# The MLP's first pair: rows for LayerNorm loaded later, LayerNorm two half steps later, weight parts in smaller portions

## The chip, the cores and the metric

The kernel runs on one core of a Trainium2 chip. The metric is device time in microseconds (us) of one execution, the median of several runs. A core has five instruction queues that run side by side and wait for each other through semaphores: TensorE (PE in the profile: matmuls; PEld is its load of the stationary operand), VectorE (DVE), ScalarE (ACT), GpSimd (POOL) and SyncE (SP, which here only issues DMA transfers). Each queue runs its instructions in order: one that waits holds up all that stand behind it on the same engine.

## The reference

A transformer block with S = 2048 tokens, D = 640 features, F = 1728 hidden features, all in float32. Attention is linear attention; after it comes the MLP, which is where the change lies. Cut to what matters:

```python
x = x + ga * attention(layernorm(x) * (1 + ca) + sa)
h = layernorm(x) * (1 + cb) + sb
r = relu(h @ w1 + b1)
x = x + gb * ((r * r) @ w2 + b2)
```

`sa, ca, ga, sb, cb, gb` are six rows made from a conditioning vector.

## The kernel before

**Tiles.** The 2048 tokens are 8 pairs `j` of two tiles of 128 tokens; the F features are 14 blocks `f` of 128 (the last one 64), taken two at a time in 7 steps `n`. Every float32 operand of a matmul is split into a high and a low part (`hi`, a copy on ScalarE, and `lo`, a subtraction on VectorE, line 88), and each product is made of three matmuls.

**The MLP loop.** For every pair and step it runs two half steps. The half step `2n` has `up(j, 2n)` (15 matmuls of `w1` with the normed tokens, into PSUM), then ScalarE's relu with bias (line 1184) and VectorE's square (line 1185); then `down(0)`, the first half of the products of the step before with `w2`. The half step `2n+1` has `up(j, 2n+1)`, relu, square, then `split_a` (lines 1208 and 1214 on ScalarE, line 88 on VectorE), which writes the split activations `ra`, then `down(1)`. So a `down` of step `n` reads the `ra` that the half step before it made. The order on all engines is the order of this code: pairs 0 and 1 are written with a manual schedule, which in pair 0 holds for SP too.

**Weight parts.** While pair 0 runs, the rest of the weights is still being loaded and split. The list `preps` has 28 parts, numbered from 0 in its order (blocks of `w1` and `w2` in turn; 14 is w1_9, 15 w2_5, 16 w1_10, 17 w2_6, 18 w1_11, 19 w2_7, 20 w1_12, 21 w2_8, 22 w1_13, 23 w2_9, 24 to 27 w2_10 to w2_13). When the MLP begins, 14 are loaded and 9 are split. `prep(n)`, called once in every half step with the next number of `PREPS`, does for the next `n` parts: the high copy on ScalarE (line 953), the low subtraction on VectorE (line 88), and issues `n` further loads on SP (lines 943 and 946, 320 KB each). The raw rows lie in a ring `s1` of five buffers, so a load waits until VectorE is done with an older row. The split weights of w1_13 (part 22) have no place of their own and take a buffer of the same ring.

**LayerNorm of the next pair.** `layer(j + 1, at)` is called in every half step `at` of pair `j` and runs what a table lists for it. For pair 1 the table is `LN_AT0`. Its entries: `load` is the half step in which SP issues the two loads of attention's rows (`xm`, line 1005) and, unless `xx` says otherwise, the two of x's rows (`xx`, line 1015), 320 KB each; `add` the half steps of the two additions on VectorE (line 1019; SP then stores the sum, line 1020); `ln` the half steps of six pieces on ScalarE: two sums (line 1418), two sums of squares (line 1423), two scalings (line 1430), with small POOL instructions between them (lines 1420 to 1427); and the keys 10, 11 and 12 the half steps in which TensorE transposes the normed tokens (`t2`, line 364, output `tb`) and ScalarE and VectorE scale and split them (lines 375, 376, 88) for pair 1's `up`. The PSUM tile that `tb` goes to exists once. In an even half step of pair 0, `t2`, loads and additions stand between `down(0)` and `prep`, and the pieces of `ln` behind `prep`; in an odd one all of `layer` stands behind `prep`.

Of the kernel before, what the change touches and what calls it, by code (L numbers as in the profile page):

```python
# [51 lines left out]
def kernel(  # L52
# [1210 lines left out]
    def t_split(n):  # L1263

        a, b = TR_[n]
        for r, w in (("a", a[:, L]), ("b", TR_[n, "b"][:, 1].bitcast(F32)), ("c", b[:, L]), (None, b[:, R])):
            if r == "b":
                t = TR_[n, "b"]
            elif r and n == NP - 2:
                at = 512 if r == "a" else 1280  # L1270
                t = TR_["end"][:, at : at + 768].rearrange("p (s n) -> p s n", s=2)
            else:
                t = ring(r, f"tst{n}_{r}") if r else W2[2 * n][:, :, R]
            nc.scalar.activation(t[:, 0], w, AF.Copy)
            lo(t[:, 1], w, t[:, 0])
            if r:
                nc.sync.dma_start(TD[n][r], t.bitcast(F32))
# [121 lines left out]
    def prep(n):  # L1399
        p_hi(n)  # L1400
        p_lo(n)
        p_load(n)
# [1 line left out]
    prev = None  # L1404
    LN2 = {}

    LN_AT0 = {"load": 1, "add": (4, 5), "ln": (4, 5, 6, 7, 8, 9), 10: (0, 1), 11: (2, 3), 12: (4,)}
    LN_AT1 = {"load": 3, "add": (5, 5), "ln": (5, 6, 6, 7, 8, 8), 9: (0, 1), 11: (2, 3), 12: (4,)}
    LN_AT2 = {"load": 0, "xx": 3, "add": (6, 7), "ln": (7, 8, 8, 8, 9, 9), 10: (0, 1), 11: (2, 3), 12: (4,)}
    LN_AT = {"load": 0, "add": (3, 4), "ln": (4, 5, 6, 6, 7, 7), 8: (0, 1), 10: (2, 3), 12: (4,)}  # L1410
    PREPS = iter([1, 3] + [2, 2] * 2 + [2, 1] * 2 + [1])

    def ln_pieces(xt, nm, spare):
        sm = small([P, 2], "sm", f"sm{nm}")
# [18 lines left out]
    def layer(j, at, part=None):  # L1433
        todo = {1: LN_AT0, PLAIN: LN_AT1, PLAIN + 1: LN_AT2}.get(j, LN_AT)
        if j == NB:
            return
        if part != 1:
            if at in todo:
                t2(j, *todo[at])
            if todo["load"] == at:  # L1440
                load_xm(j)
            if todo.get("xx", todo["load"]) == at:
                load_xx(j)
            for i in range(2):
                if todo["add"][i] == at:
                    add_x(j, i)
        if part == 0:
            return
        for i in range(6):
            if todo["ln"][i] == at:  # L1450
                if i == 0:
                    LN2[j] = ln_pieces(XM[j], f"b{j}", XX[j])
                next(LN2[j])

    for j in range(NB):
# [5 lines left out]
        for n in range(NP):  # L1461
# [16 lines left out]
            if j >= PLAIN:  # L1478
# [3 lines left out]
                layer(j + 1, 2 * n)  # L1482
            prep(next(PREPS, 0))
            if j == 0:
# [44 lines left out]
            if m == NP + 1:  # L1529
                t_split(NP - 2)  # L1530
            prep(next(PREPS, 0))
            if n == 0 and j:
# [77 lines left out]
```

## Time and profile before

| what | value |
|---|---|
| time, median of 3 runs | 780.56 us (780.42 to 780.70) |
| the profiled execution | 780.88 us, of which the span from first to last instruction is 779.2 us |
| mean clock granted to TensorE | 0.999 of full speed |
| share of VectorE, ScalarE, POOL busy | 75%, 56%, 16% |

The profile is one execution. A row of a timeline gives the start in us from the span's start, the length in us, the engine, the line of the kernel, the operation, output and inputs by their names (numbers left out), the shape, and how many instructions were merged (x15); in brackets stands how long the engine was idle before it and what released it. An SPq row is the issue of a transfer, not its flight. A row "a <- b: total, times, longest" is a wait; a row that begins with A:B is a stretch of time with the busy us of PE, PEld, DVE, ACT and POOL, then the granted clock, the share in which the DMA engines were busy and the GB/s they moved; a row of DMA issues ends with the size of one transfer and the us from its issue to its landing.

### The profile page before, as it was taken

To read this page: it belongs to the slowest core of one execution; us is meant where nothing else is said; L and a number is where in the kernel's file an instruction comes from. 1 tells how busy PE (TensorE), PEld (TensorE's weight loads), DVE (VectorE), ACT (ScalarE), POOL (GpSimd) and SP (SyncE) were. 2 spreads that over 40 slices of the span, in tenths; PEclk is the share of its full clock that TensorE was granted. 3 is DMA by queue.
4 is the path that set the end of the run, shared out by engine and by line. 5 is a ranking of instruction groups with operands and counts; after the bars stand their busy time and mean duration, and the time that the engine had idled before them with its cause. 6 is when DMAs were issued, how large, how long until landed. Compare 5 with 4: busy or idle time off the path is not lost.

```text
span 779.2 us, 15296 instructions
## 1 busy us (share of the span) xinstructions
PE 769.2 (99%) x5989; PEld 745.3 (96%) x5989; DVE 584.8 (75%) x1059; ACT 440.2 (56%) x991; POOL 122.5 (16%) x253
## 2 busy tenths in 40 slices
PE   9999999999999999999998999999999999999997
PEld 9999999999999989998998999999999999999997
DVE  6699899998788799986265567776857567586656
ACT  5766775485753365656776637547464645536331
POOL 3001101001100232320000101122131313213110
PEclk9999999999999999999999999999999999999999
DMA  8713254432130245222247346898666868666450
GB/s 333 290 68 131 84 158 154 135 110 94 69 102 2 101 153 170 85 94 94 96 140 256 119 159 240 270 322 244 194 195 209 235 186 255 185 196 205 130 174 34
DMA packets 50552, 126.03 MB, mean 162 GB/s; under 512 B 5992, under 2 KB 6760, under 8 KB 50480
## 3 DMA queue, kind: packets, MB, share of 16 engines
q1 hardware_dynamic: 33144, 83.99, 31.2%
q0 software_dynamic: 14752, 35.76, 16.6%
q10 hardware_dynamic: 2583, 5.30, 1.8%
q8 instruction: 47, 0.77, 0.4%
q14 instruction: 26, 0.20, 0.1%
HBM read 95.05 MB, written 29.88 MB: 160 GB/s over the span
## 4 chain that ended last, share of the span: by engine, by line
PE 94%; ACT 2%; DVE 1%; DMA 1%; issue 1%; POOL 0%; DVEq 0%; ACTq 0%; POOLq 0%
PE up L78 22%; PE acc L78 16%; PE pwo L78 10%; PE pq L78 9%; PE pk L78 9%; PE pv L78 9%; PE acc3x L78 5%; PE kvp L448 3%; PE te L865 2%; PE tb L364 1%; PE numa L78 1%; PE foldk L280 1%; DMA rw<-in_w 1%; PE numc L78 1%; PE numb L78 1%; PE ta L364 1%
## 5 line engine op out<-in xcount | busy, mean ns | idle before, releaser
L78 PE MATMUL up<-h,w 128*128 128x256 f32 x1640 | 206.5, 278 | 0.2 <-ACT ft L1184 0.2
L78 PEld LDWEIGHTS up<-h,w 128*128 128x128 f32 x1640 | 196.1, 188 | 0.3 <-ACT ft L1184 0.3
L1184 ACT ACTIVATE ft<-up,b_t 128x256 f32<-128x256 f32 x104 | 49.1, 472 | 112.0 <-PE up L78 111.4
L78 PE MATMUL acc<-w,ra 128*128 128x384 f32 x452 | 98.5, 336 | 2.7 <-ACT ra L1208 2.7
L1185 DVE TENSOR_TENSOR ft<-ft 128x256 f32<-128x256 f32 x104 | 44.0, 424 | 50.7 <-ACT ft L1184 49.0
L78 PE MATMUL pwo<-wo,ot 128*128 128x256 f32 (+3 forms) x512 | 81.1, 312 | 0.0
L78 PE MATMUL pk<-wk,hT 128*128 128x384 f32 (+1 forms) x480 | 77.7, 311 | 0.2 <-ACT hT L376 0.2
L78 PEld LDWEIGHTS pwo<-wo,ot 128*128 128x128 f32 (+1 forms) x512 | 75.0, 188 | 2.7 <-issue 2.7
L78 PEld LDWEIGHTS acc<-w,ra 128*128 128x128 f32 x452 | 72.6, 188 | 4.3 <-ACT ra L1208 3.1
L78 PE MATMUL pv<-wv,hT 128*128 128x384 f32 (+1 forms) x480 | 76.0, 310 | 0.0
L78 PE MATMUL pq<-wq,hT 128*128 128x384 f32 (+1 forms) x480 | 75.0, 311 | 0.4 <-ACT k L424 0.4
L78 PEld LDWEIGHTS pk<-wk,hT 128*128 128x128 f32 x480 | 71.8, 188 | 1.9 <-ACT hT L376 0.8
L78 PEld LDWEIGHTS pq<-wq,hT 128*128 128x128 f32 x480 | 70.8, 188 | 1.6 <-ACT k L424 0.9
L78 PEld LDWEIGHTS pv<-wv,hT 128*128 128x128 f32 x480 | 70.8, 188 | 0.4
L88 DVE TENSOR_TENSOR ra<-ft,ra 128x384 fp32r<-128x384 f32 (+2 forms) x86 | 36.8, 449 | 32.8 <-ACT ra L1208 20.2
L78 PE MATMUL acc3x<-w,ra 128*128 128x256 f32 x248 | 42.4, 278 | 0.0
L1208 ACT ACTIVATE ra<-ft 128x384 fp32r<-128x384 f32 x48 | 25.2, 526 | 28.4 <-DVE ft L1185 22.4
L78 PEld LDWEIGHTS acc3x<-w,ra 128*128 128x128 f32 x248 | 39.8, 188 | 0.2 <-DVE ra L88 0.2
L1294 POOL DMA_DIRECT2D ring_a<-td_a x34 | 18.2, 536 | 124.2 <-PE acc L78 102.3
L1199 DVE TENSOR_TENSOR ft<-ft 128x128 f32<-128x128 f32 x136 | 33.3, 286 | 1.2
L476 DVE TENSOR_REDUCE rs_q<-eq 128x64 f32<-128x1280 f32 x16 | 23.5, 1475 | 11.1 <-ACT eq L435 11.1
L88 DVE TENSOR_TENSOR h<-xx,h 128x256 fp32r<-128x256 f32 x35 | 14.9, 424 | 21.8 <-ACT h L376 21.8
(256 smaller groups left out, 1406.1 us busy)
## 6 DMA issues: line engine op xcount, KB each, us to landing
ring_c<-td_c POOLq DMA_DIRECT2D x34, 384.0 KB, 4.1
ring_a<-td_a POOLq DMA_DIRECT2D x34, 384.0 KB, 3.8
ring_b<-td_b POOLq DMA_DIRECT2D x34, 256.0 KB, 3.9
esp<-eq SPq DMA_DIRECT2D x12, 640.0 KB, 2.9
el<-esp SPq DMA_DIRECT2D x12, 640.0 KB, 3.9
rw<-in_w SPq DMA_DIRECT2D x23, 320.0 KB, 4.0
wm<-in_w_mod SPq DMA_DIRECT2D x20, 320.0 KB, 4.3
xb<-in_x SPq DMA_DIRECT2D x8, 640.0 KB, 4.0
```

Source lines behind the costliest of these rows:

```text
L78: nc.tensor.matmul(o, a, b, start=first and i == 0, stop=last and i == len(terms) - 1, skip_group_check=skip,)
L88: (eng or nc.vector).tensor_tensor(out_lo, full, hi.bitcast(F32), op=ALU.subtract)
L280: nc.tensor.matmul(p[g // 3][:, (g % 3) * 120 : (g % 3) * 120 + n], r, bd_t[:120, g * 120 : g * 120 + n], start=True, stop=True,)
L364: nc.tensor.transpose(p[:, i * P : (i + 1) * P], xn[:, i, d * P : (d + 1) * P], ident)
L448: nc.tensor.matmul(kvp[g // 4][64 * c : 64 * c + 64, a : a + 2 * n].rearrange("p (s n) -> p s n", s=2), v[:, u], e[:, :, o : o + n], start ...
L476: nc.vector.tensor_reduce(s, heads(flat(e)), axis=AX.X, op=ALU.add)
L865: nc.tensor.transpose(p[:m, a : a + P], EU[2 * j + i][:, b : b + m], ident)
L1184: nc.scalar.activation(r, p, AF.Relu, bias=b1_t[:, f : f + 1])
L1185: nc.vector.tensor_tensor(r, r, r, op=ALU.mult)
L1199: nc.vector.tensor_tensor(t[:, o], t[:, a], t[:, b], op=op)
L1208: nc.scalar.activation(a[:, 0, :3], t[:, :3], AF.Copy)
L1294: nc.gpsimd.dma_start(RING[j, n, r], TD[n][r].bitcast(F32R))
```

## The change

Two tables of numbers. `LN_AT0`: attention's rows are loaded in half step 3 instead of 1, x's rows in 4 instead of 1; the additions run in 6 and 7 instead of 4 and 5; the six pieces of LayerNorm in 6, 7, 8, 8, 9, 9 instead of 4 to 9. The transposes stay in 10, 11 and 12. `PREPS`: the 19 weight parts that are left go to the half steps 0 to 11 as 1, 3, 2, 1, 2, 1, 2, 2, 1, 1, 1, 2, where they went to 0 to 10 as 1, 3, 2, 2, 2, 2, 2, 1, 2, 1, 1.

```diff
-    LN_AT0 = {"load": 1, "add": (4, 5), "ln": (4, 5, 6, 7, 8, 9), 10: (0, 1), 11: (2, 3), 12: (4,)}
+    LN_AT0 = {"load": 3, "xx": 4, "add": (6, 7), "ln": (6, 7, 8, 8, 9, 9), 10: (0, 1), 11: (2, 3), 12: (4,)}
...
-    PREPS = iter([1, 3] + [2, 2] * 2 + [2, 1] * 2 + [1])
+    PREPS = iter([1, 3] + [2, 1] * 2 + [2, 2] + [1, 1] + [1, 2])
```

## The prediction

> **What bounds the kernel.** I read the page first, then TensorE's waits, then the timelines of TensorE, ScalarE, VectorE and the SP queue around the stretch that the change touches.
>
> ```profile
> PE 769.2 (99%) x5989; PEld 745.3 (96%) x5989; DVE 584.8 (75%) x1059; ACT 440.2 (56%) x991; POOL 122.5 (16%) x253
> ...
> PE acc L78 <- ACT ra L1208: 2.7, 2, 1.4
> ```
>
> TensorE is busy 99% of the span, so time can only come out of its gaps, and its waits list one group worth having: two waits, 2.7 us together, for ScalarE's `ra` (the split of the activations). Both lie in pair 0 of the MLP, where the diff works:
>
> ```profile
> 408.24 1.86 PE L78 MATMUL up<-h,w 128*128 128x256 f32 x15
> ...
> 411.65 1.86 PE L78 MATMUL up<-h,w 128*128 128x256 f32 x15
> ...
> 415.07 1.86 PE L78 MATMUL up<-h,w 128*128 128x256 f32 x15
> ...
> 418.20 1.04 PE L78 MATMUL acc<-w,ra 128*128 128x384 f32 x3 [1.26 <-ACT ra L1208]
> ...
> 420.30 1.86 PE L78 MATMUL up<-h,w 128*128 128x256 f32 x15
> ...
> 423.72 1.86 PE L78 MATMUL up<-h,w 128*128 128x256 f32 x15
> ...
> 427.03 1.04 PE L78 MATMUL acc<-w,ra 128*128 128x384 f32 x3 [1.45 <-ACT ra L1208]
> ...
> 429.14 1.87 PE L78 MATMUL up<-h,w 128*128 128x256 f32 x15
> ...
> 435.99 0.60 PE L364 MATMUL tb<-ident,xm 128*128 128x128 f32 x4
> ```
>
> I number the half steps h by the `up` that opens them: the `up` rows are h4 to h9. An undisturbed half step lasts 3.42 us (408.24 to 411.65 to 415.07; 420.30 to 423.72). From h6 to h7 it is 5.23 and from h8 to h9 5.42. So the two waits really cost 1.81 + 2.00 = **3.81 us**, more than their 2.7, because the first product after each (1.04 us for three matmuls) also waits for VectorE's part of the split. That is the most that can be won.
>
> **Why ScalarE was late.**
>
> ```profile
> 408.19 1.06 SPq L943 DMA_DIRECT2D rw<-in_w  x1
> ...
> rw<-in_w SPq DMA_DIRECT2D x1, 320.0 KB, 7.1
> ...
> 410.00:412.00 2.00, 2.00 (x17) 2.00 (x17) 1.30 (x3) 1.19 (x2) 0.00 (x0) 1.00 0.89 289
> ...
> 415.32 0.74 ACT L953 ACTIVATE w<-rw 128x640 fp32r<-128x640 f32 x1 [3.93 <-DMA rw<-in_w]
> ...
> 420.49 0.82 DVE L1019 TENSOR_TENSOR xm<-xm,xx 128x640 f32<-128x640 f32 x1
> ...
> 421.34 0.74 ACT L1418 ACTIVATE xx<-xm 128x640 f32<-128x640 f32 x1 [1.73 <-DVE xm L1019]
> ...
> 422.08 0.46 ACT L1184 ACTIVATE ft<-up,b_t 128x256 f32<-128x256 f32 x1
> ...
> 422.44 0.72 ACT L953 ACTIVATE w<-rw 128x640 fp32r<-128x640 f32 x1
> ...
> 423.19 0.83 DVE L88 TENSOR_TENSOR w<-rw,w 128x640 fp32r<-128x640 f32 x1 [0.20 <-ACT w L953]
> ...
> 424.05 0.74 ACT L953 ACTIVATE w<-rw 128x640 fp32r<-128x640 f32 x1 [0.89 <-DVE w L88]
> ...
> 424.83 0.49 DVE L88 TENSOR_TENSOR w<-rw,w 128x320 fp32r<-128x320 f32 x1 [0.81 <-ACT w L953]
> ```
>
> Part 18 of the weights (counting from 0) was issued at 408.19 behind four row transfers of LayerNorm (`xm`, `xx`) and landed 7.1 us later, with the transfers at 289 GB/s. ScalarE stood 3.93 us at its copy; behind that stood relu 5 and the split that h6's `down` needed: wait one. Then a LayerNorm sum waited 1.73 us for an addition, and the copy of part 22 0.89 us for VectorE's part 21 (the buffer of w1_13 comes out of the ring of five raw rows and comes free with part 21). Relu 6 so ran at 422.08, five us after its `up`: wait two.
>
> **The change, part by part.** No instruction and no byte is added or removed: the same 19 weight parts are split, in 12 portions where there were 11. Only order moves.
>
> *Loads.* `xm` moves from h1 to h3 and `xx` to h4, so part 18 no longer stands behind four 320 KB transfers (1.31 MB, 4.5 us at 289 GB/s): it should land near 415.3 - 4.5 = 410.8. Its copy moves from h4 to h5, about 415.2. The 3.93 us are gone, with 4 us of cover. SP now runs part 20, `xm` twice, `xx` twice, then parts 21 and 22:
>
> ```profile
> 409.40 1.56 DVE L88 TENSOR_TENSOR w<-rw,w 128x640 fp32r<-128x640 f32 x2
> ...
> 406.25 0.90 SPq L1005 DMA_DIRECT2D xm<-a  x2
> ...
> 407.24 0.85 SPq L1015 DMA_DIRECT2D xx<-in_x  x2
> ...
> xx<-in_x SPq DMA_DIRECT2D x2, 320.0 KB, 6.6
> ```
>
> Part 20 takes the row that part 15 frees at the half of the VectorE row, 410.2; with SP's spacing the last `xx` is issued near 412.0. At 6.6 us, slow as before, the rows are there by 418.1 and 418.6. The first addition (h6) can start at 417.8 and its sum has 1 us before relu 7; the second (h7) is due only at 424.8 (below). Parts 21 and 22 wait on SP behind `xx`, go out at 412.2 and 412.9, and are wanted at 422.0 and 423.6. So lateness here costs nothing up to 6 us.
>
> The Trainium skill ("DMA: Bandwidth & Descriptors", § Rules for kernel authors) says to issue a DMA early and wait for it late, which speaks against this move. The trace has the counterexample: the early rows were what part 18 waited behind. By the row the two old waits go and the sum keeps their 3.81 us; by the rule VectorE would wait for the late rows and the time would rise, to 783 in the case worked out as the last rival.
>
> *h6.* Without the stall relu 5 starts at 413.6, its split is ready at 415.1 (1.47 after the relu, as 425.51 to 426.98 below) and h6's `down` is due half a half step, 1.71, after 415.07, at 416.8: 1.81 us come back. h7 begins at 415.07 + 3.42 = 418.49. *h8.* Relu 7 starts 1.95 after its `up` (408.24 to the relu at 410.19, below) at 420.44, split ready at 421.9, due at 423.6: 2.00 us come back.
>
> *The new tight place.* From h7 on ScalarE has a chain without slack, which ends at LayerNorm's last piece, now in h9, and the transposes in h10 read it. Steps from these rows and those above:
>
> ```profile
> 410.19 0.48 ACT L1184 ACTIVATE ft<-up,b_t 128x256 f32<-128x256 f32 x1 [0.20 <-PE up L78]
> ...
> 425.51 0.46 ACT L1184 ACTIVATE ft<-up,b_t 128x256 f32<-128x256 f32 x1
> ...
> 426.46 0.52 ACT L1208 ACTIVATE ra<-ft 128x384 fp32r<-128x384 f32 x1 [0.49 <-DVE ft L1185]
> ...
> 427.08 0.72 ACT L953 ACTIVATE w<-rw 128x640 fp32r<-128x640 f32 x1
> ...
> 427.71 0.81 ACT L1423 ACTIVATE xx<-xm,smb 128x640 f32<-128x640 f32 x1
> ...
> 428.52 0.45 ACT L1184 ACTIVATE ft<-up,b_t 128x256 f32<-128x256 f32 x1
> ...
> 430.56 0.92 ACT L1430 ACTIVATE xm<-xm,nbb,sqb 128x640 f32<-128x640 f32 x1 [0.32 <-POOL nbb L1427]
> ...
> 431.38 0.46 ACT L1184 ACTIVATE ft<-up,b_t 128x256 f32<-128x256 f32 x1
> ```
>
> Relu 7 to copy 21: 1.57 (425.51 to 427.08). Copy 21 to VectorE's part 21: 0.75. Then copy 22: 0.86. Then VectorE's part 22: 0.78. Then the second addition: 0.41 (0.49 less the overlap of rows that follow each other; here is the 424.8). Addition to sum: 0.85. Sum to relu 8: 0.74. Relu 8 to copy 23: 0.36. Copy to square: 0.63. Two squares: 0.81 each. Relu 9 to copy 24: 1.57. Copy to the first scaling: 0.63. Scaling: 0.82, the last 0.92 to its end. Sum 12.51; with 1.95 ahead and 0.02 behind, 14.48 us after h7 begins: **432.97**. TensorE would be there at 418.49 + 4 x 3.42 = 432.17. So the transposes wait about **0.8 us**. (Relu 9's split is ready at 418.49 + 11.99, due at + 11.97: at most 0.4 us of a wait, which the later 0.8 swallows. POOL's constants come 2.04 us after the last square's end, 428.52 to 430.56, just within the 1.57 + 0.63 = 2.20 until the first scaling.)
>
> Before, these transposes ran at 435.99; now 432.97: **3.0 us** earlier, 3.81 - 0.8.
>
> *After it.* Parts 26 and 27 now stand in h11 ahead of the transposed rows' scaling. I count from the first transposes (435.99 = 0).
>
> ```profile
> 441.03 0.55 ACT L375 ACTIVATE xx<-tb,cols_b 128x256 f32<-128x256 f32 x1
> ...
> 441.94 0.55 ACT L375 ACTIVATE xx<-tb,cols_b 128x256 f32<-128x256 f32 x1
> ...
> 443.82 0.38 PE L364 MATMUL tb<-ident,xm 128*128 128x128 f32 x2
> ...
> 448.64 0.68 PE L78 MATMUL acc<-w,ra 128*128 128x384 f32 x3
> ...
> 447.89 0.98 DVE L88 TENSOR_TENSOR ra<-ft,ra 128x128 fp32r<-128x128 f32 x3
> ```
>
> Two copies put the scalings from +5.04 and +5.95 to +6.31 and +7.22, the second done at +7.77; the last transposes, which need the same PSUM tile, are due at +7.83. So they fit with nothing over; I take 0 and keep 0.3 for the range. VectorE's last split before pair 1's first `down` (+12.65) moves from +11.9 to about +12.1 (relu 12, and with it VectorE's next work, starts that much later) and still fits. If that cover were gone, each us would count in full. From there pair 1 runs as before, earlier by the same amount.
>
> **The sum.** The profiled execution has a span of 779.2 and took 780.88, 0.32 over the median. 779.2 - 3.0 = 776.2 of span, 777.9 as run, and against the median 780.56 - 3.0 = **777.6 us**.
>
> **Rivals.** *The tight place isn't there.* If w1_13's buffer comes free earlier (the ring gives it another row), the chain is shorter by some 0.9, the transposes don't wait, and all 3.81 return: 776.8. Against it: five raw rows are taken at that copy as before. 0.18. *One wait stays*, for the chain has no slack and 2 us more on it (a load or POOL's constants late) puts the price of one old wait back: 778.6 to 778.8. For it: the two margins of 0.1 and 0.2 us above. 0.10. *The change doesn't do what it says*: ScalarE's work from h4 to h11 is the same, and the waits only move on to h10 and h12 at full size: 780.5. Against it: of the 32 us from 404 to 436 ScalarE was busy only two thirds, as the row below shows. 0.06. *Slower:* the rows of x land late. The place is the second addition, due at 424.8; beyond that every us goes down the chain to the transposes. At 427.8 the gain is used up; at 430.5, 18 us after issue, the kernel takes 783. Against it: the slowest landing seen here is 7.1 us. 0.04.
>
> ```profile
> 404.00:436.00 32.00, 29.29 (x225) 28.30 (x224) 20.68 (x36) 21.23 (x43) 2.51 (x5) 1.00 0.66 218
> ```
>
> **How the numbers follow.** My forecast has 0.60, with its own range 776.9 to 778.2; the rest (0.02) is unnamed. The range 776.6 to 778.9 takes in the first two rivals and leaves out the last two. Within 0.2% (1.56 us, about what a measurement can tell here) means 779.0 to 782.1: the idle rival and a little, 0.08. Slower 0.04. Faster 0.88.
>
> **What will show it.** Right: the waits of `acc` for `ra` at h6 and h8 are gone, no copy of L953 waits for a DMA, `up` rows 3.42 apart from h4 to h9, and one new wait of TensorE, the transposes in h10 for L1430 of ScalarE, about 0.8 us, with copy 22 still waiting for VectorE. The transposes begin 3.0 us earlier. Wrong: a wait of VectorE's L1019 for `xx` at h7, a wait at the last transposes, or `up` rows in pair 1 that shift by another amount than the first transposes.

## The result and the profile after

| kernel | median, lowest to highest | span of the profiled execution |
|---|---|---|
| before | 780.50 us, 779.97 to 781.01 (10 runs) | 779.2 us |
| changed | 778.47 us, 778.17 to 779.06 (10 runs) | 776.8 us |

The ratio is 0.9973 with a 95% interval of 0.9965 to 0.9981: between 1.5 and 2.7 us faster. Forecast were 777.6, so the direction and the place were right and the gain, 2.0 us by the medians and 2.47 by the trace (below), came out smaller than the 3.0 that were worked out. 778.47 lies 0.27 above the forecast's own range (776.9 to 778.2) and inside the wider one (776.6 to 778.9). After the change, TensorE's list of waits has one of the MLP's first pair (total, times, longest), and its timeline shows where (start, length, engine; in brackets the idle time and its releaser):

```profile
PE tb L364 <- ACT xm L1430: 0.6, 1, 0.6
```

```profile
404.90 1.86 PE L78 MATMUL up<-h,w 128*128 128x256 f32 x15
...
415.16 1.86 PE L78 MATMUL up<-h,w 128*128 128x256 f32 x15
...
418.58 1.86 PE L78 MATMUL up<-h,w 128*128 128x256 f32 x15
...
428.84 1.86 PE L78 MATMUL up<-h,w 128*128 128x256 f32 x15
430.61 1.03 PE L78 MATMUL acc<-w,ra 128*128 128x384 f32 x3
...
432.71 0.27 PE L364 MATMUL tb<-ident,xm 128*128 128x128 f32 x1
433.63 0.55 PE L364 MATMUL tb<-ident,xm 128*128 128x128 f32 x3 [0.65 <-ACT xm L1430]
433.93 1.97 PE L78 MATMUL up<-h,w 128*128 128x256 f32 x15
...
444.56 1.86 PE L78 MATMUL up<-h,w 128*128 128x256 f32 x15
```

From the `up` of h3 (404.90) to that of h10 (428.84) seven half steps take 23.94 us, 3.42 each: both old waits are gone. The new loss is all in h10. Undisturbed, the `up` of h11 would begin 3.42 + 0.36 (transposes) after 428.84, at 432.62; it begins at 433.93, **1.31 us** late. So 3.81 came back and 1.31 went again, 2.50 (the ruler below has 2.47; the other 0.03 lie behind the `up` of h11).

The same stretch in the kernel before:

```profile
404.81 1.86 PE L78 MATMUL up<-h,w 128*128 128x256 f32 x15
...
446.94 1.86 PE L78 MATMUL up<-h,w 128*128 128x256 f32 x15
```

I use the distance from the `up` of h3 to the first `up` of pair 1 as a ruler: 446.94 - 404.81 = 42.13 us before, 444.56 - 404.90 = 39.66 after, 42.13 - 3.81 = 38.32 with no wait left. It is needed because the `up` of h3 itself begins anywhere from 404.31 to 404.92 in the profiles of this study, and not by what the kernels change: those with the rows loaded in h1 begin between 404.31 and 404.81, those with the rows later between 404.59 and 404.92. A whole span carries these 0.6 us along.

The chain of waits says where h10 went (start, length, what ran or was waited for):

```profile
426.56 0.36 ACT ft L1184
426.93 0.63 ACT w L953
427.56 0.02 issue
427.58 0.84 DVE w L88
428.42 0.02 issue
428.44 0.57 SPq L946
429.01 0.05 issue
429.06 0.58 SPq L946
429.64 0.05 issue
429.69 2.88 DMA x<-xm
432.57 0.02 issue
...
432.66 0.93 ACT xm L1430
433.59 0.04 issue
433.63 0.55 PE tb L364 x3
```

Read it upwards. The transposes waited for the second scaling (L1430). That began at 432.66 because a transfer `x<-xm` had just landed: the store of the summed row (line 1020), which reads the very row that the scaling overwrites. The store was issued only at 429.69, though its addition was done at 425.7, because two transfers of L946 stood ahead of it on SP (part 27, 64 rows twice), and these waited for VectorE to be done with part 23 (427.58 to 428.42), whose row they take. On ScalarE it looks like this:

```profile
431.29 0.91 ACT L1430 ACTIVATE xm<-xm,nbb,sqb 128x640 f32<-128x640 f32 x1
432.66 0.92 ACT L1430 ACTIVATE xm<-xm,nbb,sqb 128x640 f32<-128x640 f32 x1 [0.46 <-DMA x<-xm]
```

### The profile page after: what moved, and what is told of

The parts are those of the page before. It is cut to its first block, busy times and chain, and to the rows that moved or that the text cites. A ratio compares the mean times of both kernels' runs of the same rounds, so it can differ in the third digit from the quotient of the medians.

```text
span 776.8 us, 15295 instructions
## 1 busy us (share of the span) xinstructions
PE 768.9 (99%) x5989; PEld 745.3 (96%) x5989; DVE 585.0 (75%) x1059; ACT 440.3 (57%) x991; POOL 123.9 (16%) x253
## 4 chain that ended last, share of the span: by engine, by line
PE 96%; ACT 2%; DVE 1%; DMA 0%; issue 0%; SPq 0%; POOL 0%; ACTq 0%; POOLq 0%
PE up L78 23%; PE acc L78 17%; PE pwo L78 10%; PE pq L78 9%; PE pk L78 9%; PE pv L78 9%; PE acc3x L78 5%; PE kvp L448 3%; PE te L865 2%; PE tb L364 1%; PE numa L78 1%; PE foldk L280 1%; PE numc L78 1%; PE numb L78 1%; PE ta L364 1%; PE foldq L280 1%
## 5 line engine op out<-in xcount | busy, mean ns | idle before, releaser
L828 POOL TENSOR_TENSOR dn<-dn,rs_q 128x64 f32<-128x64 f32 x16 | 8.7, 543 | 131.1 <-DVE dn L826 131.1
```

## The experiments

Each is timed beside the kernel before on the same chip, whose medians there were 780.41 (first four experiments) and 780.82 us (last three); "ruler" is the distance above, from the one profiled execution of each kernel, with its two ends.

| kernel | median | ratio to before, 95% | ruler | from, to |
|---|---|---|---|---|
| before | 780.50 | | 42.13 | 404.81, 446.94 |
| changed | 778.47 | 0.9973, 0.9965 to 0.9981 | 39.66 | 404.90, 444.56 |
| store ahead of two loads | 777.62 | 0.9963, 0.9950 to 0.9975 | 39.09 | 404.59, 443.68 |
| LayerNorm's table alone | 778.28 | 0.9973, 0.9962 to 0.9984 | 38.82 | 404.92, 443.74 |
| portions alone | 777.85 | 0.9968, 0.9956 to 0.9981 | 39.82 | 404.37, 444.19 |
| changed, rows in h1 | 778.26 | 0.9975, 0.9965 to 0.9984 | 39.64 | 404.31, 443.95 |
| LayerNorm's places new, rows in h1, old portions | 780.15 | 0.9992, 0.9983 to 1.0001 | 41.47 | 404.55, 446.02 |
| new portions, rows in h1, LayerNorm one half step later | 777.42 | 0.9957, 0.9945 to 0.9970 | 38.34 | 404.60, 442.94 |
| store ahead, part 21 in h6 | 777.02 | 0.9956, 0.9943 to 0.9968 | 38.33 | 404.68, 443.01 |

The intervals overlap in most pairs, so the verdicts between experiments rest on the ruler and on the waits. The gain by the ruler lies inside the interval of the ratio in every row but one, LayerNorm's table alone.

**Does the store set the end?** In half step 7 only, the loads go behind `layer`:

```diff
-            prep(next(PREPS, 0))
+            k2 = next(PREPS, 0)
+            p_hi(k2)
+            p_lo(k2)
+            if (j, n) != (0, 3):
+                p_load(k2)
...
             layer(j + 1, 2 * n + 1)
+            if (j, n) == (0, 3):
+                p_load(k2)
```

> The changed kernel, but in half step 7 the loads of parts 26 and 27 are issued on SP behind LayerNorm's store of the second summed row instead of ahead of it. Theory (store): the second scaling waits for that store, which stood behind load 27 and so behind VectorE's part 23; now the store goes out near 425.7, no wait of L1430 for a DMA is left (0.46 before), the scaling ends near 433.0, the next up begins near 433.4 instead of 433.93: time 777.9 to 778.0. Rival (ScalarE's chain is just longer than counted, the store only happens to end there): the up stays at 433.9, time 778.5.

SP's, ScalarE's and TensorE's timelines of this kernel:

```profile
425.41 0.33 SPq L1020 DMA_DIRECT2D x<-xm  x1
425.84 3.48 SPq L946 DMA_DIRECT2D rw<-in_w  x3
```

```profile
430.98 1.72 ACT L1430 ACTIVATE xm<-xm,nbb,sqb 128x640 f32<-128x640 f32 x2
```

```profile
404.59 1.86 PE L78 MATMUL up<-h,w 128*128 128x256 f32 x15
...
432.37 0.93 PE L364 MATMUL tb<-ident,xm 128*128 128x128 f32 x4
433.05 2.02 PE L78 MATMUL up<-h,w 128*128 128x256 f32 x15
...
443.68 1.86 PE L78 MATMUL up<-h,w 128*128 128x256 f32 x15
```

The store is out at 425.41, the two scalings follow each other without a gap, and the ruler falls by 0.57 to 39.09. The rival, a ScalarE chain that is longer of itself, is out. What is left, 39.09 - 38.32 = 0.77 us, is what the prediction had for the whole of the new wait (0.8). The median, 777.62, is even 0.3 below the 777.9 to 778.0 expected.

**Which half of the change pays?** First the new `LN_AT0` with the old `PREPS`:

```diff
-    PREPS = iter([1, 3] + [2, 1] * 2 + [2, 2] + [1, 1] + [1, 2])
+    PREPS = iter([1, 3] + [2, 2] * 2 + [2, 1] * 2 + [1])
```

> New LN_AT0, old PREPS: rows and LayerNorm later, weight parts in the old portions. Theory (store): loads 26 and 27 are issued one half step earlier, ahead of the second addition, so the store isn't held up; ScalarE's chain reaches relu 9 near 428.9, hardly earlier than in the changed kernel (429.08), the second scaling isn't held, the up after the transposes begins near 433.2: time 777.7. Rival (the new portions are what frees ScalarE): a wait of acc for ra stays at h6 or h8, time 779 or more.

TensorE's, ScalarE's and SP's timelines of this kernel:

```profile
432.47 0.92 PE L364 MATMUL tb<-ident,xm 128*128 128x128 f32 x4
433.14 1.96 PE L78 MATMUL up<-h,w 128*128 128x256 f32 x15
```

```profile
431.06 1.72 ACT L1430 ACTIVATE xm<-xm,nbb,sqb 128x640 f32<-128x640 f32 x2
```

```profile
420.87 4.45 SPq L946 DMA_DIRECT2D rw<-in_w  x3
425.37 0.58 SPq L1020 DMA_DIRECT2D x<-xm  x1
```

The ruler is 38.82: no listed wait of TensorE is left in the pair, and the `up` after the transposes begins at 433.14, 0.50 us later than without any loss. Here loads 26 and 27 belong to h6, so the store goes out at 425.37, early enough for the two scalings to follow each other. The rival is out: no wait at h6 or h8. By the ruler the later loads and LayerNorm alone win 3.3 of the 3.8 us, more than the whole change. The times don't confirm that much: the median, 778.28, is above the 777.7 expected, and the interval of the ratio stands for 1.2 to 3.0 us. The profiled execution was the fastest of the seven (777.66), and nothing on record shows where the others lost time; whether this half alone beats the whole change is so shown by the trace only.

Then the old `LN_AT0` with the new `PREPS`:

```diff
-    LN_AT0 = {"load": 3, "xx": 4, "add": (6, 7), "ln": (6, 7, 8, 8, 9, 9), 10: (0, 1), 11: (2, 3), 12: (4,)}
+    LN_AT0 = {"load": 1, "add": (4, 5), "ln": (4, 5, 6, 7, 8, 9), 10: (0, 1), 11: (2, 3), 12: (4,)}
```

> Old LN_AT0, new PREPS: rows and LayerNorm as before the change, weight parts in the new portions. Theory: part 18 again lands near 415.3, but its copy now stands in h5, behind the split, so the big wait at h6 is gone; what is left there is the addition in h4, which waits for x's rows until 413.8 and pushes the square of relu 5 to 416: about 0.5 us at h6, up to 0.4 at h8, nothing at the transposes: time 777.2 to 777.7, better than the changed kernel. Rival (the loads' move is what pays): both old waits stay nearly whole, time 779.5 to 780.5.

The waits at h6 and h8 came as expected: those half steps last 3.95 (414.63 to 418.58) and 3.67 us (422.00 to 425.67) instead of 3.42, so 0.53 and 0.25 more. A third was not foreseen, 0.69 us in h10 (4.11 us from 429.09 to the transposes at 433.20, instead of 3.42). ScalarE's and POOL's timelines show it:

```profile
428.74 0.93 ACT L1430 ACTIVATE xm<-xm,nbb,sqb 128x640 f32<-128x640 f32 x1 [0.95 <-POOL nbb L1427]
429.57 0.45 ACT L1184 ACTIVATE ft<-up,b_t 128x256 f32<-128x256 f32 x1
430.52 0.52 ACT L1208 ACTIVATE ra<-ft 128x384 fp32r<-128x384 f32 x1 [0.49 <-DVE ft L1185]
```

```profile
427.95 0.76 POOL L1427 TENSOR_TENSOR nbb<-smb,sqb 128x2 f32<-128x2 f32 x1
```

The first scaling, in h8 only two us behind the last square, waited 0.95 us for POOL, and behind it stood relu 9 and the split for h10. So the ruler is 39.82, no better than the change (39.66), and the median, 777.85, is above the 777.2 to 777.7 expected. The rival is out all the same: part 18 was issued at 408.05 and landed 6.7 us later, as late as before, and its wait is gone, because its copy stands one half step later (416.55).

**Does it matter when the rows are loaded?** The same edit, twice: with the new portions and with the old ones.

```diff
-    LN_AT0 = {"load": 3, "xx": 4, "add": (6, 7), "ln": (6, 7, 8, 8, 9, 9), 10: (0, 1), 11: (2, 3), 12: (4,)}
+    LN_AT0 = {"load": 1, "add": (6, 7), "ln": (6, 7, 8, 8, 9, 9), 10: (0, 1), 11: (2, 3), 12: (4,)}
```

> The changed kernel, but both pairs of row loads issued in h1 as before the change. Theory: with the new portions part 18's copy stands in h5 at 415.24, and lands at 415.3, so nothing is lost: time as the changed kernel, 778.4 to 778.6, up rows equally spaced through h6. Rival (the transfers ahead of part 18 cost the first wait whatever the portions): about 1.8 us come back, 780.2.

With the new portions: 39.64, as the change to 0.02 us, and the same wait of the second scaling for the store:

```profile
432.07 0.92 ACT L1430 ACTIVATE xm<-xm,nbb,sqb 128x640 f32<-128x640 f32 x1 [0.47 <-DMA x<-xm]
```

The later loads win nothing here.

> New LayerNorm places, old PREPS, row loads in h1 as before the change. Theory: in the old portions part 18 is copied in h4, three us ahead of its landing at 415.3, so the early rows cost the first wait (about 1.4 us at h6), and ScalarE, late from there, makes most of the rest too: first up of pair 1 about 41.8 us after the up of h3 (42.13 before the change, 38.82 with the rows later), time 779.5 to 780.3. Rival (the place of the row loads doesn't matter with old portions either): as with the rows later, 38.8 us, 778.3.

With the old portions TensorE's timeline has waits again:

```profile
417.65 1.04 PE L78 MATMUL acc<-w,ra 128*128 128x384 f32 x3 [0.98 <-ACT ra L1208]
...
432.66 1.04 PE L78 MATMUL acc<-w,ra 128*128 128x384 f32 x3 [0.53 <-ACT ra L1208]
```

ScalarE waits 4.0 us for raw rows, 3.62 of them at the copy of part 18; the ruler is 41.47 against 38.82 with the rows later, and the time can't be told from that of the kernel before (0.67 us less by the medians, with 1.0001 still in the interval). So the two halves of the change are two remedies for one trouble, part 18 wanted ahead of its landing: bring it earlier, or want it later. Each alone takes most of the loss away (3.3 and 2.3 of 3.8 us by the ruler); both together gain no more, and together they made the store's new wait, since the portions put loads 26 and 27 into the half step of the second addition.

**What takes the rest away?** Two kernels, each against another part of the chain. The first has the new portions, the rows in h1, and LayerNorm one half step later than before instead of two:

```diff
-    LN_AT0 = {"load": 3, "xx": 4, "add": (6, 7), "ln": (6, 7, 8, 8, 9, 9), 10: (0, 1), 11: (2, 3), 12: (4,)}
+    LN_AT0 = {"load": 1, "add": (5, 6), "ln": (5, 6, 7, 8, 9, 9), 10: (0, 1), 11: (2, 3), 12: (4,)}
```

> The changed PREPS, row loads in h1, LayerNorm one half step later than before the change instead of two (additions in 5 and 6, pieces in 5, 6, 7, 8, 9, 9). Theory: the new portions leave ScalarE free enough; the second addition now stands ahead of part 22 and its store goes out at once; the last scaling ends near 431.2, a us before TensorE comes to the transposes, and no wait is left: 38.3 to 38.5 us from the up of h3 to the first up of pair 1, time 776.8 to 777.1. Rival (ScalarE has no room for an earlier LayerNorm, the delay by two half steps is needed): waits of acc for ra at h6 or h8, 39.5 us or more, time 778 or more.

The second keeps the change's table, has the store ahead of the loads, and splits part 21 in h6 (the loads stay), so that copy 22 needn't wait for it:

```diff
-            prep(next(PREPS, 0))
+            k1 = next(PREPS, 0)
+            extra = 1 if (j, n) == (0, 3) else 0
+            p_hi(k1 + extra)
+            p_lo(k1 + extra)
+            p_load(k1)
...
-            p_hi(k2)
-            p_lo(k2)
+            p_hi(k2 - extra)
+            p_lo(k2 - extra)
```

> The changed kernel with the store issued ahead of loads 26 and 27, and part 21 split in h6 instead of h7, its loads as they were. It takes the wait of copy 22 for part 21 (0.89 us) and copy 21 itself off ScalarE's chain. Theory: the chain from relu 7 to the transposes gets 1.6 us shorter, the 0.76 us that are left with the store alone go away: 38.3 to 38.5 us from the up of h3 to the first up of pair 1, time 776.8 to 777.1. Rival (the wait for the buffer is covered, something else sets the transposes): 39.1 us as with the store alone, 777.6.

TensorE's timelines, first the one with LayerNorm earlier, then the one with part 21 earlier:

```profile
428.54 1.86 PE L78 MATMUL up<-h,w 128*128 128x256 f32 x15
...
431.96 0.60 PE L364 MATMUL tb<-ident,xm 128*128 128x128 f32 x4
432.32 1.96 PE L78 MATMUL up<-h,w 128*128 128x256 f32 x15
```

```profile
428.62 1.86 PE L78 MATMUL up<-h,w 128*128 128x256 f32 x15
...
432.05 0.60 PE L364 MATMUL tb<-ident,xm 128*128 128x128 f32 x4
432.40 1.96 PE L78 MATMUL up<-h,w 128*128 128x256 f32 x15
```

Both reach the transposes 3.42 and 3.43 us after the `up` of h10 and go on without a gap: rulers 38.34 and 38.33, the 38.32 of a pair with no wait. The second shows that copy 21 and the buffer wait of copy 22, taken off the chain together, were enough for the rest of its excess; it doesn't tell the two apart. Their medians, 777.42 and 777.02, are the lowest of the study (the first is 0.3 above the 776.8 to 777.1 expected, the second within), and by the ratios the two are 0.43 and 0.44% under the kernel before; the change was 0.27% under it.

## Why the prediction was right, and where it was off

- *Both old waits return, 3.81 us.* Right: 3.42 us from `up` to `up` through h10.
- *The loads.* Right in what they cover: no copy waits for a DMA and no addition for the rows of x. The first of these rows landed 5.2 us after its issue at 411.67, 1.1 us ahead of its addition (417.97), where the prediction, with 6.6, had it land 0.3 us behind the 417.8 it gave for that addition. The rule of the Trainium skill ("DMA: Bandwidth & Descriptors", § Rules for kernel authors), to issue early and wait late, doesn't decide here. With the new portions early and late rows give the same ruler (39.64 and 39.66 us); with the old ones early rows cost 2.65 (41.47 - 38.82), because part 18, which is wanted sooner, lands behind them.
- *The tight chain from relu 7.* Right up to its last but one step. The prediction has the first scaling 1.95 + 10.77 after h7 begins; from 418.58 that is 431.30, and it began at 431.29. The buffer wait of copy 22 was there (0.89 us).
- *The split of relu 9.* As said, at most 0.4 us, inside the larger wait: the first products of h10 began 0.07 us late (430.61) and took 1.03 us instead of 0.68, 0.43 in all by the product after them.
- *The step that failed* is "Scaling: 0.82". It lets the second scaling follow the first as if only ScalarE's own order held it. It also waits for the store of its row, which moved too, past other things on SP: the additions of h7 stand behind `prep`, and `prep` now issues loads 26 and 27 there. The prediction followed SP's queue for the row loads and for parts 20 to 22, not for line 1020. The step measured 432.66 - 431.29 = 1.37 instead of 0.82, 0.55 more, and the experiment with the store ahead gave 0.57 back. With it the new loss comes to 0.8 + 0.55 = 1.35; the trace has 1.31.
- *Behind it.* The last transposes had no wait: ScalarE's scalings ahead of them were done at 441.33 and they began at 441.42, 0.09 us to spare where the prediction had 0.06. Pair 1 followed at the same spacing, to 0.03 us.
- *Among the rivals*, the result lies toward "one wait stays" (778.6), and its price was near, but not its reasons: neither a load nor POOL's constants were late for ScalarE. That the stated range, which was drawn to take in this rival, holds the result is so far luck; the forecast's own range doesn't hold it. "The tight place isn't there" was wrong, since the ring did give w1_13 the row of part 21. "The rows of x land late" did not happen: in the changed kernel no addition waited for them. (With the rows in h1 and the additions in h4 and h5 the first addition did wait, 2.46 us in the kernel before and 2.57 with the portions alone.)

## What to carry to other kernels

When a step that works in place is moved, list everything that still reads the buffer, stores too, and see what each of those now stands behind on its own queue: a store that nobody waits for becomes part of the path when its source is overwritten. Two remedies for one wait don't add up, and the second can make a wait of its own; try each alone. Where single waits of less than a microsecond count, compare the distance between two instructions around the change rather than whole spans.

## What the runs showed of the hardware that was not expected

POOL's small product of two columns (L1427), on the same shape each time, took 0.76 us for pair 1 in the kernel before and with the portions alone, and 0.19 or 0.20 us in the other seven kernels. Where it took 0.76, a VectorE subtraction of 128x640 had begun just ahead of it, and it ended 0.06 us behind that subtraction with the portions alone (428.65 to 428.71). Where it took 0.19 or 0.20, VectorE was idle at that moment. The rows, VectorE and POOL of the kernel before, then POOL of the changed one:

```profile
429.64 1.56 DVE L88 TENSOR_TENSOR w<-rw,w 128x640 fp32r<-128x640 f32 x2 [0.20 <-ACT w L953]
...
429.77 0.76 POOL L1427 TENSOR_TENSOR nbb<-smb,sqb 128x2 f32<-128x2 f32 x1
```

```profile
430.32 0.20 POOL L1427 TENSOR_TENSOR nbb<-smb,sqb 128x2 f32<-128x2 f32 x1
```

A later pair of the kernel before has a third length, 0.41 us, behind a shorter VectorE instruction; again POOL ends 0.05 us after it:

```profile
566.56 0.43 DVE L1185 TENSOR_TENSOR ft<-ft 128x256 f32<-128x256 f32 x1 [1.99 <-ACT ft L1184]
...
566.63 0.41 POOL L1427 TENSOR_TENSOR nbb<-smb,sqb 128x2 f32<-128x2 f32 x1
```

The Trainium skill ("GPSIMD Engine Reference", § 1. Specifications) says that POOL's SBUF interfaces are shared with VectorE, with contention where a VectorE instruction has two SBUF inputs, as this subtraction does. The rows agree, but no run was made to test it by itself. In the changed kernel POOL's constants so came 0.6 us sooner than the prediction allowed for, which widened one of its margins and moved nothing. With the portions alone it mattered: of the 0.95 us for which the first scaling waited, 0.56 are the difference between the two lengths (an estimate, 0.76 - 0.20).
